# One softmax block left in PSUM, and one weight split in fixed slots, in an attention-and-Fourier kernel

## The chip, the cores and the metric

One core of a Trainium2 chip. A core has a matrix engine (TensorE), three engines for elementwise work (VectorE, ScalarE and GpSimd), a SyncE queue that issues the DMAs, and two on-chip memories: SBUF, and PSUM, whose banks take the results of TensorE. Each engine runs its own list of instructions in order; engines wait for one another by semaphores. In the profile the engines are called PE (PEld for its weight loads), DVE, ACT, POOL and SP.

The metric is the device time of one execution in microseconds (us), less is better.

## What is computed

Two independent halves, whose results stand side by side in the output. `x` has 2048 rows and 576 columns in each.

```python
# A: attention with 32 heads of 18 columns, in 4 segments of 512 rows
for s in range(4):
    logits = einsum("bhqd,bhkd->bhqk", qs, ks) * scale + mask   # causal in the segment
    p = softmax(logits)
    a_dot = einsum("bhqk,bhkd->bhqd", p, vs)
    a_mem = (phi(qs) @ M) / (phi(qs) @ z + 1e-6)                # memory of earlier segments
    o = g * a_mem + (1 - g) * a_dot
    M, z = M + phi(ks).T @ vs, z + phi(ks).sum()
a = concat(o) @ wo
# B: real part of a two-dimensional Fourier transform by matrices
y = Cr @ (x @ Hr.T) - Ci @ (x @ Hi.T)
```

`Hr` and `Hi` (576x576) are the first and the second transform along the columns, `Cr` and `Ci` (2048x2048) along the rows.

## The kernel before the change

**Precision by splitting.** Most operands are held as two parts, a rounded `hi` and the rest `lo = raw - hi`. ScalarE makes `hi` by a copy, VectorE or GpSimd subtracts, and TensorE adds the products `hi*hi`, `hi*lo` and `lo*hi`.

**Stages.** Up to about 215 us the projections and the memories of the segments are computed. Then one long stage, until about 928 us, runs attention (`attention()`) and the Fourier half (`dense()`) side by side: both are generators that yield after a piece of work. The main loop takes one slot of attention, runs what is due, and then takes pieces of `dense()` until its share of planned time has caught up. Last comes the output projection.

**Order of the work.** The order of instructions on each engine is the order in which the program emits them; nothing reorders it. `later(n, fn)` emits `fn` after `n` further ticks of a clock, and the main loop ticks once a slot. `PLAN` maps a slot's number (8 times the pair and the slot in the pair) to functions that are emitted there, behind that slot's own work; `at(p, slot, fn)` in `right_operands` fills it, before the change for the output projection's operands alone.

**A pair.** Attention handles two heads in one pass of its loop over `p` (64 pairs, 8 slots each). It works as a pipeline: pass `p` starts the row minima of pair `p` and goes on with pairs `p-2`, `p-3` and `p-4` (`F_LAG`, `T_LAG`, `V_LAG`). A block triangle of 4x4 blocks is computed in three pieces, `kind` 0, 1 and 2.

- Even head: `s_fill` computes scores and VectorE takes the row minima (line 973). Later `t_fill` computes the transposed scores with these minima added, and ScalarE takes exponentials. For `kind` 1 and 2 it does so twice from the same PSUM bank: `hi` in 16 bits (L1053) and `f` in 32 bits (L1054). For `kind` 0 GpSimd masks `f` first. `t_lo` (L1068) makes `lo = f - hi`: VectorE for `kind` 0 and 1, GpSimd for `kind` 2. `pv` multiplies by the values.
- Odd head: `f_fill` computes scores and minima in one go, `f_exp` takes exponentials (L996), `f_split_hi` and `f_split_lo` (L1003, L1007) split them into `hl`, and `f_turn` transposes `hl` into `ptt` by a DMA (L1012), which `pv` uses a pass later.

**PSUM banks.** `bank()` hands out two banks with tag `s` and two with tag `t`, each in turn. In a pass the tag `t` is taken four times: `t_fill` kind 0, 1 and 2, and `f_fill` kind 0. So `f_fill` kind 0 gets the bank that `t_fill` kind 1 had, and `t_fill` kind 1 of the next pass the one that `f_fill` kind 0 had. The tag `s` goes round `s_fill` 0, 1, 2 and `f_fill` 1, 2. A matmul into a bank waits until the readers of its last contents are done.

**Order in a pass, on VectorE:** `t_lo` 0 of the even head behind it, `s_fill` 0, `s_fill` 1, `f_split_lo` (512 columns), `s_fill` 2, `f_fill` 1, `f_fill` 0, `f_fill` 2, `t_lo` 1, then `pv_out` (L1098 to L1107). The middle block's exponentials stand in the tile `pf` in SBUF between L1054 and L1068.

**The second transform's weights.** `dense()` first makes the column transforms of the 16 row tiles with `Hr` (`hidden`, L94), then 16 row transforms (`sequence`, L583 and L628 to L633), then the same with `Hi`. `Hi` comes in five blocks of 128 rows. In the first row transforms `h_load(1, k)` loads block `k` (L425), and one `sequence` later `h_split(1, k)` makes its parts through `split_wk`: copies on ScalarE (L130), and two ticks later the subtractions on VectorE (L124, or L126 and L127 for the last block, which has two halves of 64 rows).

**Row maxima.** `maxima`, `maxima_transpose` and two small DMAs (`qs<-mt`) bring the minima of the even heads into the operand of the transposed scores.

Of the kernel before, what the change touches and what calls it, by code (L numbers as in the profile page):

```python
# [12 lines left out]
F32 = mybir.dt.float32  # L13
# [3 lines left out]
AF = mybir.ActivationFunctionType  # L17
OP = mybir.AluOpType
# [7 lines left out]
SCALE = DH ** -0.5  # L26
LOWEST = -3.0e38
LIFT = 12.0 * math.log(2.0)
# [12 lines left out]
def infini_attention_and_fnet(ctx: ExitStack, tc: tile.TileContext, xT, wqk, w8, wv, wo, beta, xtT, cT, hT, out):  # L41
    nc = tc.nc
    act, dve, pool, pe = nc.scalar, nc.vector, nc.gpsimd, nc.tensor
# [44 lines left out]
    def later(n, fn, *a):  # L88
        due.setdefault(clock[0] + n, []).append((fn, a))
# [28 lines left out]
            act.activation(t, raw, AF.Copy)  # L118
            dve.tensor_tensor(t[64:], raw[64:], t[64:].bitcast(F32), OP.subtract)

    def split_wk(w, k, raw, wait=0):
        def low():
            if k < 4:
                dve.tensor_tensor(w[1][k], raw, w[0][k].bitcast(F32), OP.subtract)  # L124
            else:
                dve.tensor_tensor(w[2][:64], raw[:64], w[2][:64].bitcast(F32), OP.subtract)  # L126
                dve.tensor_tensor(w[3][64:], raw[64:], w[3][64:].bitcast(F32), OP.subtract)  # L127

        for t in (w[0][k],) if k < 4 else (w[2], w[3]):
            act.activation(t, raw, AF.Copy)  # L130
        if wait:
            later(wait, low)
        else:
            low()

    def load_w(src, cols, k):
        raw = sb.tile([P, cols], F32, name="raw", tag="raw", bufs=5)
        dma(raw, src[k])
        return raw

    def weight(mk):
        return [[mk() for _ in range(4)] for _ in range(2)] + [mk() for _ in range(2)]

    def wide_tile(cols):
        return lambda: wide.tile([P, cols], F32R, name="wide", tag="wide")
# [17 lines left out]
    raw = sb.tile([P, L], F32, name="raw", tag="raw", bufs=5)  # L163
# [8 lines left out]
    for k in range(1, 5):  # L172
        load_x(0, k)
        raw = load_w(wqk[:, :, :L], L, k)
# [6 lines left out]
    for k in range(5):  # L181
        if k < 2:
            raw = sb.tile([P, L], F32, name="r", tag="r", bufs=3)
            dma(raw, wqk[k, :, L:])
        else:
            raw = load_w(wqk[:, :, L:], L, k)
# [234 lines left out]
    HW, HRAW = {}, {}  # L421

    def h_load(ri, k):
        HRAW[ri, k] = sb.tile([P, D], F32, name="raw", tag="raw", bufs=5 if ri == 0 else 3)
        dma(HRAW[ri, k], hT[ri, k])  # L425

    def h_split(ri, k):
        if k == 0:
            HW[ri] = weight(wide_tile(D))
        split_wk(HW[ri], k, HRAW.pop((ri, k)), 2 * ri)  # L430

    c_raw, c_split, c_seen = {}, {}, set()
    CHUNKS = [c for ri in range(2) for c in
# [29 lines left out]
    def stacks(p_, i):  # L463
        qs_bufs.append(p_.tile([P, 4, L], BF16, name=f"qs{i}"))
        ks_bufs.append(p_.tile([P, 4, L], BF16, name=f"ks{i}"))
        pool.memset(ks_bufs[i].bitcast(F32)[96:], BF16_ONES)
# [97 lines left out]
    def bank(name, shape, dtype, tag):  # L564
        turns[tag] ^= 1
        return ps.tile(shape, dtype, name=name, tag=f"{tag}{turns[tag]}", bufs=1)
# [43 lines left out]
    def y_load(tt):  # L610
        if tt < NT:
            Y[tt] = sb.tile([P, D], F32, name="y", bufs=3)
            dma(Y[tt], yd[tt])
# [54 lines left out]
    def dense():  # L668
        for ri in range(2):
            for tt in range(NT):  # L670
                yield from hidden(ri, tt)
            if ri:
                y_load(0)
            for tt in range(NT):
                late = tt - 8
                if ri == 0 and 0 <= late < 5:
                    h_load(1, late)
                if ri == 0 and 1 <= late < 6:
                    h_split(1, late - 1)
                yield from sequence(ri, tt)  # L680

    O, LEFT, WO, TAIL = {}, {}, {}, {}
# [11 lines left out]
            else:  # L694
                o_load(t, lambda: sr.tile([P, 5, P], F32, name="craw", bufs=4))

    PLAN = {}

    def right_operands():
        raw, late = {}, {}  # L700

        def at(p, slot, fn, *a):
            PLAN.setdefault(8 * p + slot, []).append((fn, a))

        def load(k):
            raw[k] = wide.tile([P, D], F32, name="wide", tag="wide") if k == 3 else sb.tile([P, D], F32, name="raw", tag="raw", bufs=3)
            dma(raw[k], wo[k])
# [241 lines left out]

    sq = ctx.enter_context(tc.tile_pool(name="sb2q", bufs=1, side="right", reuse_waits="tile"))  # L950
    sa = ctx.enter_context(tc.tile_pool(name="sb2a", bufs=1, reuse_waits="tile"))
    PT, PV = {}, {}

# [74 lines left out]
    def t_fill(n, kind, maxima_of=None):  # L1030
        G, h = divmod(n, 4)
        q, k = qs_bufs[G % 4][:NPAIR + 3, h], ks_bufs[G % 4][:NPAIR + 3, h]
        if kind == 0:
            PT[n] = (sa.tile([P, 1280], F16, name="phi", bufs=2), sa.tile([P, 1280], F16, name="plo", bufs=2),
                     sa.tile([P, 1280], F32, name="pf", bufs=3))
        hi, lo, f = PT[n]
        o = bank("t", [P, L], F32, "t")
        if kind == 0:
            for j in range(4):
                b = slice(j * P, (j + 1) * P)  # L1040
                pe.matmul(o[:, b], k[:, b], q[:, b], start=True, stop=True)  # L1041
            r, w = 0, 512
        elif kind == 1:
            pe.matmul(o[:, :384], k[:, :128], q[:, 128:], start=True, stop=True)
            if maxima_of is not None:
                maxima_transpose(maxima_of, o)
            r, w = 512, 384
        else:
            pe.matmul(o[:, 256:384], k[:, 256:384], q[:, 384:], start=True, stop=True)
            pe.matmul(o[:, :256], k[:, 128:256], q[:, 256:], start=True, stop=True)  # L1050
            r, w = 896, 384
        if kind:
            act.activation(hi[:, r:r + w], o[:, :w], AF.Exp, bias=LIFT, scale=SCALE)  # L1053
        act.activation(f[:, r:r + w], o[:, :w], AF.Exp, bias=LIFT, scale=SCALE)  # L1054

    def t_mask(n):
        v = PT[n][2][:, :512].rearrange("p (j q) -> p j q", j=4)
# [7 lines left out]
    def t_lo(n, kind):  # L1065
        hi, lo, f = PT[n]
        a, b = ((0, 512), (512, 896), (896, 1280))[kind]
        (pool if kind == 2 else dve).tensor_tensor(lo[:, a:b], f[:, a:b], hi[:, a:b], OP.subtract)  # L1068

    def pv(n):  # L1070
        G, h = divmod(n, 4)
# [71 lines left out]
    F_LAG, T_LAG, V_LAG = 2, 3, 4  # L1143
# [3 lines left out]
    def attention():  # L1147
        for p in range(NP + V_LAG):
            def even(lag, fn, *a):
                if 0 <= p - lag < NP:  # L1150
                    fn(2 * (p - lag), *a)

            def odd(lag, fn, *a):
                if 0 <= p - lag < NP:
                    fn(2 * (p - lag) + 1, *a)

            if p < 2:
                OG.append(sa.tile([P, 4, 72], F32, name=f"og{p}"))
            if p == 0:
                stack_load(1)  # L1160
                later(20, value_load, 0)
            if p % 2 == 0:
                later(39, value_load, p // 2 + 1)
                later(30, memory_load, p // 2)
            even(T_LAG + 1, t_lo, 0)
            odd(F_LAG + 1, f_exp, 2)
            odd(F_LAG + 1, f_split_hi)
            yield SLOTS[0]
            G = p // 2 - 1 if p % 2 == 0 and 0 < p <= NP else None
            even(0, s_fill, 0)  # L1170
            even(T_LAG, t_fill, 0)
            even(T_LAG, t_fill, 1, G)
            if G is not None and p < T_LAG:
                maxima_transpose(G, bank("trm", [P, L], F32, "t"))
            odd(F_LAG + 1, f_split_lo, pool, 512, 1280)
            yield SLOTS[1]
            even(0, s_fill, 1)
            odd(F_LAG + 1, f_split_lo, dve, 0, 512)
            yield SLOTS[2]
            even(V_LAG, pv)  # L1180
            if p < 2:
                stacks(sq, p + 2)
            even(0, s_fill, 2)
            even(T_LAG, t_mask)
            yield SLOTS[3]
            odd(F_LAG, f_fill, 1)
            even(T_LAG, t_fill, 2)
            odd(F_LAG, f_fill, 0)
            if p % 2 and p < NP:
                maxima(p // 2)  # L1190
            yield SLOTS[4]
            odd(F_LAG + 1, f_turn)
            if p % 2:
                if p == 1:
                    later(6, stack_load, 2)
                else:
                    stack_load((p + 3) // 2)
                if 2 < p < 18:
                    later(2, copy_parts, 2, 7 + p // 2)
            elif 4 <= p < 36:  # L1200
                later(2, copy_parts, 3, (p - 4) // 2)
            even(T_LAG, t_hi)
            yield SLOTS[5]
            odd(V_LAG, pv)
            odd(F_LAG, f_fill, 2)
            odd(F_LAG, f_exp, 1)
            even(T_LAG, t_lo, 1)
            even(T_LAG, t_lo, 2)
            yield SLOTS[6]
            odd(F_LAG, f_exp, 0)  # L1210
            if V_LAG <= p < NP + V_LAG - 1:
                pv_out(p - V_LAG)
            yield SLOTS[7]
# [8 lines left out]
    for n, w in enumerate(attention()):  # L1222
        tick()
        ta += w
        for fn, a in PLAN.pop(n, ()):
            fn(*a)
# [61 lines left out]
```

## Time and profile before

| | us |
|---|---|
| median of 3 runs | 988.1 |
| the three runs | 987.11, 988.10, 988.16 |
| the profiled execution | 987.47 |
| its span, first to last instruction | 985.7 |

Busy times of all engines, in stretches of the span (us):

| stretch | TensorE | VectorE | ScalarE | GpSimd | DMA share |
|---|---|---|---|---|---|
| 0 to 215 | 213.9 | 145.3 | 144.1 | 137.6 | 0.63 |
| 215 to 400 | 185.0 | 135.1 | 137.8 | 129.0 | 0.80 |
| 400 to 575 | 174.9 | 151.0 | 141.0 | 126.5 | 0.99 |
| 575 to 660 | 85.0 | 69.3 | 69.0 | 61.6 | 0.80 |
| 660 to 880 | 218.4 | 200.7 | 168.3 | 164.8 | 1.00 |
| 880 to 985 | 101.4 | 84.7 | 54.2 | 56.3 | 0.65 |

A row of a group reads: line, engine, operation, what it writes and reads, shape, count | busy time in us and mean ns of one | idle time of the engine just before it and what ended that. A row of a timeline reads: start in us, duration in us, engine, line, operation; in brackets the idle time before it. A row of one line's instructions gives minimum, median and maximum in ns. The matmuls of TensorE overlap, and their ends are modelled, so the distance from one start to the next says more than a duration.

### The profile page before, as it was taken

The page shows a single profiled execution, that of the slowest core. Times are in us where ns is not written, and L with a number is a line of the kernel's source. Part 1 is how long each engine was busy: PE and PEld are TensorE (multiplying, and loading weights), DVE is VectorE, ACT ScalarE, POOL GpSimd, SP SyncE. Part 2 cuts the span into 40 slices and gives each one's busy share as a digit, 9 for nine tenths or more (in the row PEclk, how much of TensorE's full clock was granted, in tenths as well). Part 3 has the DMA queues.
Part 4 walks back from the last instruction along what each step waited for, and adds up shares of the span by engine and source line. Part 5 has one row for each costly group of instructions (what it writes and reads, how often), then busy time and mean ns, then how long its engine had stood idle before and what let it go on. Part 6 is the DMA issues. An engine that isn't in the chain of part 4 may idle for free.

```text
span 985.7 us, 25490 instructions
## 1 busy us (share of the span) xinstructions
PE 978.7 (99%) x9246; PEld 917.6 (93%) x9246; DVE 786.1 (80%) x2113; ACT 714.3 (72%) x1687; POOL 675.7 (69%) x746
## 2 busy tenths in 40 slices
PE   9999999999999999999999999999999999999998
PEld 8989989899999999999999999999999989999998
DVE  6657668594678777887898888888888999999885
ACT  6757576664887877878878788886778867778442
POOL 2658577686767677666776777767677977767561
PEclk9999999999999999999999999999999999999999
DMA  7537557766778898899999997779999999988663
GB/s 237 199 117 238 203 172 249 239 238 189 185 186 218 206 253 221 214 236 237 243 239 229 228 217 189 186 199 217 239 220 247 242 225 257 233 200 191 169 197 116
DMA packets 304350, 209.96 MB, mean 213 GB/s; under 512 B 204992, under 2 KB 259136, under 8 KB 304192
## 3 DMA queue, kind: packets, MB, share of 16 engines
q1 hardware_dynamic: 304000, 208.20, 82.1%
q8 instruction: 72, 1.18, 0.5%
q14 instruction: 54, 0.44, 0.2%
q10 hardware_dynamic: 224, 0.14, 0.0%
HBM read 122.37 MB, written 58.98 MB: 184 GB/s over the span
## 4 chain that ended last, share of the span: by engine, by line
PE 94%; DVE 3%; DMA 1%; ACT 1%; issue 1%; POOL 0%; SPq 0%
PE d L583 38%; PE s L967 7%; PE v L84 6%; PE qk L84 6%; PE qk L250 6%; PE pv L1085 4%; PE d L628 3%; PE d L629 3%; PE d L630 3%; PE t L867 2%; PE pv L1086 2%; PE d L867 2%; PE s L867 1%; PE m L363 1%; PE t L1041 1%; PE look L396 1%
## 5 line engine op out<-in xcount | busy, mean ns | idle before, releaser
L973 DVE CUSTOM_DVE_ANT_0 s<-s,causal 128x128 f32<-128x128 f32 (+3 forms) x512 | 248.3, 503 | 90.9 <-PE s L967 80.8
L456 POOL TENSOR_TENSOR clo<-craw,chi 128x512 fp32r<-128x512 f32 x159 | 220.9, 1389 | 86.8 <-ACT chi L451 61.0
L583 PE MATMUL d<-wide,chi 128*128 128x288 f32 x1408 | 261.8, 303 | 0.0
L583 PEld LDWEIGHTS d<-wide,chi 128*128 128x128 f32 x1408 | 210.6, 188 | 2.3 <-issue 0.9
L583 PE MATMUL d<-wide,clo 128*128 128x288 f32 x704 | 173.2, 313 | 0.0
L1007 POOL TENSOR_TENSOR hl<-pf,hl 128x768 f16<-128x768 f32 x64 | 112.6, 1759 | 63.8 <-ACT hl L1003 53.7
L967 PE MATMUL s<-ks,qs 108*128 108x128 bf16 (+3 forms) x512 | 132.9, 303 | 1.1 <-DVE negm L973 1.1
L1053 ACT ACTIVATE phi<-t 128x384 f16<-128x384 f32 x128 | 61.7, 482 | 99.7 <-PE t L1050 99.7
L996 ACT ACTIVATE pf<-s,nb 128x128 f32<-128x128 f32 (+3 forms) x256 | 128.3, 527 | 6.2
L1068 DVE TENSOR_TENSOR plo<-pf,phi 128x384 f16<-128x384 f32 (+1 forms) x128 | 124.8, 975 | 0.0
L583 PE MATMUL d<-ab,chi 128*128 128x288 f32 x640 | 123.3, 302 | 0.0
L583 PEld LDWEIGHTS d<-wide,clo 128*128 128x128 f32 x704 | 117.8, 189 | 1.9 <-issue 0.4
L1054 ACT ACTIVATE pf<-t 128x384 f32<-128x384 f32 (+1 forms) x192 | 99.4, 518 | 6.5 <-PE t L1041 6.3
L451 ACT ACTIVATE chi<-craw 128x512 fp32r<-128x512 f32 x160 | 100.2, 627 | 4.5 <-DMA craw<-cT 2.8
L583 PEld LDWEIGHTS d<-ab,chi 128*128 128x128 f32 x640 | 97.8, 188 | 0.5
L1003 ACT ACTIVATE hl<-pf 128x768 f16<-128x768 f32 (+1 forms) x128 | 87.4, 730 | 2.0
L583 PE MATMUL d<-ab,clo 128*128 128x288 f32 x320 | 83.0, 308 | 0.0
L628 PE MATMUL d<-wide,chi 128*128 128x288 f32 x256 | 81.4, 318 | 0.0
L629 PE MATMUL d<-wide,chi 128*128 128x288 f32 x256 | 75.6, 295 | 0.0
L630 PE MATMUL d<-wide,clo 128*128 128x288 f32 x256 | 75.5, 295 | 0.0
L1068 POOL TENSOR_TENSOR plo<-pf,phi 128x384 f16<-128x384 f32 x64 | 62.3, 974 | 14.9 <-ACT pf L1054 10.8
L1007 DVE TENSOR_TENSOR hl<-pf,hl 128x512 f16<-128x512 f32 x64 | 68.3, 1068 | 0.0
(285 smaller groups left out, 2518.8 us busy)
## 6 DMA issues: line engine op xcount, KB each, us to landing
craw<-cT SPq DMA_DIRECT2D x128, 256.0 KB
ks<-kd SPq DMA_DIRECT2D x32, 432.0 KB
qs<-qd SPq DMA_DIRECT2D x32, 432.0 KB
craw<-xtT SPq DMA_DIRECT2D x32, 320.0 KB
vd<-vs SPq DMA_DIRECT2D x16, 440.0 KB
vst<-vd SPq DMA_DIRECT2D x32, 220.0 KB
qd<-p SPq DMA_DIRECT2D x16, 384.0 KB
kd<-p SPq DMA_DIRECT2D x16, 384.0 KB
```

The source lines that it names most:

```text
L84: pe.matmul(o, a, b, start=n == 0, stop=n == len(terms) - 1)
L451: act.activation(hi, raw[:, :4], AF.Copy)
L456: engine.tensor_tensor(lo, raw[:, :4], hi.bitcast(F32), OP.subtract)
L583: pe.matmul(o[h], a, b[:, h * 288:h * 288 + 288], start=start, stop=stop)
L628: pe.matmul(o, xh[:, k], wl[k][:, cs], start=k == 0, stop=False)
L629: pe.matmul(o, xh[:, k], wh[k][:, cs], start=False, stop=False)
L630: pe.matmul(o, xl[:, k], wh[k][:, cs], start=False, stop=False)
L967: pe.matmul(o[:, c:c + w], q[:, i * P:w], k[:, :w], start=True, stop=True)
L973: dve.tensor_tensor_reduce(o[:, c:c + w], o[:, c:c + w], CAUSAL[0][:, L - w:], scale=scale, scalar=-LOWEST, op0=OP.add, op1=OP.min, accum_ ...
L996: act.activation(f[:, FIRST_COL[i]:FIRST_COL[i] + w], o[:, c:c + w], AF.Exp, bias=nb[:, i:i + 1], scale=-1.0)
L1007: engine.tensor_tensor(hl[:, 1, a:b], f[:, a:b], hl[:, 0, a:b], OP.subtract)
L1068: (pool if kind == 2 else dve).tensor_tensor(lo[:, a:b], f[:, a:b], hi[:, a:b], OP.subtract)
```

## The change

It has two parts.

The middle block: for `kind` 1, ScalarE writes the 32-bit exponentials over the scores in their PSUM bank instead of into `pf`, and `t_lo` 1 reads them there. The call of `t_lo` 1 moves from behind `f_fill` 2 to behind `s_fill` 1 of the same pass.

The weights: `h_split(1, k)` is no longer called from `dense()`; it stands in `PLAN` at slot 2 of pairs 21, 23, 25, 27 and 29. The subtraction follows three ticks later, and for the last block the second half's eight ticks after the first half's. The loads stay where they were. For the first transform (`ri` 0) and for all other weights `split_wk` emits the same as before.

```diff
-    def split_wk(w, k, raw, wait=0):
-        def low():
+    def split_wk(w, k, raw, planned=False):
+        def low(i):
             if k < 4:
                 dve.tensor_tensor(w[1][k], raw, w[0][k].bitcast(F32), OP.subtract)
             else:
-                dve.tensor_tensor(w[2][:64], raw[:64], w[2][:64].bitcast(F32), OP.subtract)
-                dve.tensor_tensor(w[3][64:], raw[64:], w[3][64:].bitcast(F32), OP.subtract)
+                r = slice(64 * i, 64 * i + 64)
+                dve.tensor_tensor(w[2 + i][r], raw[r], w[2 + i][r].bitcast(F32), OP.subtract)
...
-        if wait:
-            later(wait, low)
-        else:
-            low()
+        for i in range(1 + k // 4):
+            if planned:
+                later(3 + 8 * i, low, i)
+            else:
+                low(i)
...
-        split_wk(HW[ri], k, HRAW.pop((ri, k)), 2 * ri)
+        split_wk(HW[ri], k, HRAW.pop((ri, k)), ri)
...
-                if ri == 0 and 1 <= late < 6:
-                    h_split(1, late - 1)
                 yield from sequence(ri, tt)
...
-    PLAN = {}
+    PLAN, HW1 = {}, 21
...
+        for k in range(5):
+            at(HW1 + 2 * k, 2, h_split, 1, k)
...
-        act.activation(f[:, r:r + w], o[:, :w], AF.Exp, bias=LIFT, scale=SCALE)
+        to = f[:, r:r + w]
+        if kind == 1:
+            to = KEPT[n] = o[:, :w]
+        act.activation(to, o[:, :w], AF.Exp, bias=LIFT, scale=SCALE)
...
-        (pool if kind == 2 else dve).tensor_tensor(lo[:, a:b], f[:, a:b], hi[:, a:b], OP.subtract)
+        f = KEPT.pop(n) if kind == 1 else f[:, a:b]
+        (pool if kind == 2 else dve).tensor_tensor(lo[:, a:b], f, hi[:, a:b], OP.subtract)
...
             even(0, s_fill, 1)
+            even(T_LAG, t_lo, 1)
             odd(F_LAG + 1, f_split_lo, dve, 0, 512)
...
             odd(F_LAG, f_exp, 1)
-            even(T_LAG, t_lo, 1)
             even(T_LAG, t_lo, 2)
```

More of the change, by code (lines that the diff above doesn't have):

```diff
@@ L951, in infini_attention_and_fnet @@
     sa = ctx.enter_context(tc.tile_pool(name="sb2a", bufs=1, reuse_waits="tile"))
-    PT, PV = {}, {}
+    PT, PV, KEPT = {}, {}, {}
     ROWS = (((3, 0),), ((0, 384), (2, 0)), ((1, 0),))
```

## The prediction

> **What bounds the kernel now.** I read the page first, for the engine that has no room, then the waits of TensorE, then single steps of its timeline.
>
> ```profile
> span 985.7 us, 25490 instructions
> PE 978.7 (99%) x9246; PEld 917.6 (93%) x9246; DVE 786.1 (80%) x2113; ACT 714.3 (72%) x1687; POOL 675.7 (69%) x746
> PE 94%; DVE 3%; DMA 1%; ACT 1%; issue 1%; POOL 0%; SPq 0%
> ...
> PE s L967 <- DVE negm L973: 1.1, 3, 0.4
> PE t L1041 <- DMA qs<-mt: 0.8, 1, 0.8
> ```
>
> TensorE is busy for 978.7 of 985.7 us and makes 94% of the chain of waits. Behind its start, only two kinds of wait are long enough to show as idle time: 1.1 us for VectorE and 0.8 us for one small DMA. The change removes no matmul, so it can shorten the program only through TensorE's waits. Idle time understates them, since ends of matmuls are modelled; starts are better. In TensorE's timeline:
>
> ```profile
> 666.12 0.18 PE L1086 MATMUL pv<-vst,plo 128*128 128x37 bf16 x1
> 666.68 0.27 PE L967 MATMUL s<-ks,qs 108*128 108x256 bf16 x1 [0.38 <-DVE negm L973]
> ...
> 810.20 0.20 PE L1085 MATMUL pv<-vst,phi 128*128 128x55 bf16 x1
> 810.39 0.19 PE L1086 MATMUL pv<-vst,plo 128*128 128x37 bf16 x1
> 810.43 0.19 PE L1085 MATMUL pv<-vst,phi 128*128 128x55 bf16 x1
> ...
> 810.87 0.18 PE L1086 MATMUL pv<-vst,plo 128*128 128x37 bf16 x1
> 811.42 0.27 PE L967 MATMUL s<-ks,qs 108*128 108x256 bf16 x1 [0.38 <-DVE negm L973]
> ...
> 862.72 0.30 PE L583 MATMUL d<-wide,chi 128*128 128x288 f32 x1
> 862.85 0.29 PE L583 MATMUL d<-wide,clo 128*128 128x288 f32 x1
> 863.19 0.38 PE L967 MATMUL s<-ks,qs 108*128 108x128 bf16 x2
> ...
> 882.84 0.18 PE L1086 MATMUL pv<-vst,plo 128*128 128x37 bf16 x1
> 883.37 0.27 PE L967 MATMUL s<-ks,qs 108*128 108x256 bf16 x1 [0.35 <-DVE negm L973]
> ```
>
> A small `pv` matmul is followed after about 0.03 us (810.39 to 810.43 is 0.04, most are less). The steps 666.12 to 666.68, 810.87 to 811.42 and 882.84 to 883.37 are 0.56, 0.55 and 0.53, so each holds about 0.5 us of waiting for VectorE's row minimum. The step 810.20 to 810.39 holds about 0.16 of waiting for `plo`. A `d` matmul takes 0.13 (862.72 to 862.85); the step to 863.19 is 0.34, 0.21 too long. Sum of what VectorE costs here: 0.53 + 0.52 + 0.50 + 0.16 + 0.21 = 1.92 us. Read the same way, I find no other wait on VectorE above 0.16 us between 215 and 930 us. The room for gain is small from the start.
>
> **VectorE's subtraction of the middle block, 64 times (`t_lo` with kind 1).** Groups by line with shapes kept apart, then single lines with minimum, median and maximum in ns:
>
> ```profile
> L1068 DVE TENSOR_TENSOR plo<-pf,phi 128x384 f16<-128x384 f32 x64 | 51.5, 804 | 0.0
> L276 DVE TENSOR_TENSOR r<-qk,p 128x512 f32<-128x512 f32 x36 | 24.6, 685 | 9.3 <-ACT p L275 7.7 <-POOL p L288 1.5
> ...
> L1054 ACT ACTIVATE pf<-t 128x384 f32<-128x384 f32 x128 | 61.9, 483 | 0.0
> ...
> L1068 DVE TENSOR_TENSOR plo<-pf,phi x128: 552/685/2164, 257.5 to 920.0; 128x384 f16<-128x384 f32 x64, 128x512 f16<-128x512 f32 x64
> L94 DVE TENSOR_TENSOR wide<-d,wide x44: 419/451/459, 221.8 to 625.3; 128x288 fp32r<-128x288 f32 x44
> ```
>
> It reads two SBUF tiles now: mean 804 ns, and the line spreads from 552 to 2164. Afterwards one operand lies in PSUM. No row of before has this form at 384 columns. L94 and L276 do, at 288 and 512, and L94 never leaves 419 to 459. Between them, 451 + 96/224 × (685 − 451) = 551 ns. Bounds: 0.45 (the shorter L94) and 0.80 (no change). I take 0.55, which is also the undisturbed minimum of today's form. So 0.25 × 64 = 16 us of VectorE's 786 go; off the path they are worth nothing.
> [...]
>
> ScalarE's write goes to PSUM: no row prices a ScalarE write there. Bounds 483 ± 130 ns, the upper above the 595 or so of 512 columns, or ± 8 us over 64 instructions. ScalarE's slack in the next fence hides it; I take nothing.
>
> **Its new place.** An ordinary pair, rows of VectorE, TensorE, ScalarE and SyncE:
>
> ```profile
> 441.05 0.14 DVE L973 DVE_READ_ACCUMULATOR2_ANT negm<- 128x1 f32 x1
> 441.05 0.70 DVE L1007 TENSOR_TENSOR hl<-pf,hl 128x512 f16<-128x512 f32 x1
> 443.85 0.14 DVE L973 DVE_READ_ACCUMULATOR2_ANT nb<- 128x1 f32 x1
> 444.95 0.43 DVE L973 CUSTOM_DVE_ANT_0 s<-s,causal 128x256 f32<-128x256 f32 x1 [0.96 <-PE s L967]
> 445.30 0.56 DVE L1068 TENSOR_TENSOR plo<-pf,phi 128x384 f16<-128x384 f32 x1
> ...
> 442.29 0.38 PE L967 MATMUL s<-ks,qs 108*128 108x512 bf16 x1
> 454.61 0.20 PE L1085 MATMUL pv<-vst,ptt 128*128 128x55 bf16 x1
> ...
> 438.98 0.50 ACT L1054 ACTIVATE pf<-t 128x384 f32<-128x384 f32 x1
> 442.49 0.49 ACT L1053 ACTIVATE phi<-t 128x384 f16<-128x384 f32 x1 [2.49 <-PE t L1050]
> 446.31 0.19 ACT L993 ACTIVATE nb<-nb 128x1 f32<-128x1 f32 x1
> ...
> 441.84 4.20 SPq L1012 DMA_TRANSPOSE ptt<-hl  x1
> ```
>
> The subtraction leaves 445.30, behind `f_fill` kind 2, and goes to 441.19, between `s_fill` kind 1 and `f_split_lo`. Its inputs are there since 439.48. Behind it wait, 0.55 later each: `f_split_lo`; the minima of `s_fill` 2, `f_fill` 1 and 0, up to 443.99; and through `hl` the transposing DMA, so SyncE's queue behind 441.84. The cover: VectorE idles 0.96 before 444.95, so the next minimum starts on time; ScalarE takes up `f_fill` 0's result only at 446.31, 2.3 us after it; the transposed block lands by about 446 and is used at 454.61. Price nothing; without cover 0.55 a pair.
>
> TensorE gets a new wait. `f_fill` kind 0 (442.29) reuses the bank with the middle block, so it must follow the subtraction instead of the exponential: 441.19 + 0.55 + about 0.06 for the signal (estimate) = 441.80, still 0.49 early. Where VectorE is late this margin shrinks:
>
> ```profile
> 661.18 1.62 DVE L1068 TENSOR_TENSOR plo<-pf,phi 128x384 f16<-128x384 f32 x1
> 805.06 1.17 DVE L1068 TENSOR_TENSOR plo<-pf,phi 128x384 f16<-128x384 f32 x1
> 884.08 0.14 DVE L973 DVE_READ_ACCUMULATOR2_ANT negm<- 128x1 f32 x1
> ...
> 884.67 0.38 PE L967 MATMUL s<-ks,qs 108*128 108x512 bf16 x1
> ```
>
> At 884 it is 0.45, below the 0.61 needed. But lateness is what the move removes: 1.62 us (661.18) and 1.17 us (805.06) of subtraction precede the stalls at 666 and 811 on VectorE's queue and would be gone before them; 0.8 on the mean elsewhere, more than any stall above. I take all 1.92 us off, and add 0.3 for new waits (bounds 0 and 1.2, the shortfalls of the 9 of 61 pairs whose margin is under 0.61, as at 884, if VectorE were no earlier at all).
>
> **The second transform's weights.** Same six ScalarE copies and six VectorE subtractions; their loads stay in the transform's loop.
>
> ```profile
> 520.79 1.25 ACT L130 ACTIVATE wide<-raw 128x576 fp32r<-128x576 f32 x2
> ...
> L124 DVE TENSOR_TENSOR wide<-raw,wide x4: 751/1690/1831, 452.1 to 505.0; 128x576 fp32r<-128x576 f32 x4
> ...
> 430.71 0.41 SPq L425 DMA_DIRECT2D raw<-hT  x1
> ```
>
> The copies come after pair 21's first scores, about 440, 9 us after the first load, and lie in front of 442.49, where ScalarE idles 2.49 us: 1.25 is hidden. The subtractions move to just before `f_fill` 2, where 0.96 us is idle: of 1.83 at most 0.87 spills over, against 0.80 that left the place behind it. Splitting the last block parts 2 × 1.5 us. None of the five stalls lies among 452 to 526, so I take nothing: bounds −0.3 (small waits) to +0.5 (one stall as at 666).
>
> **Sum.** Profiled execution 987.47 us (span 985.7 and 1.8 around it): 987.47 − 1.92 + 0.3 = 985.85. The median of the runs is 0.63 above this execution, their lowest value 0.36 below it; with half of the offset, 986.1.
>
> **Rivals.** First, **the waits are dealt anew**: VectorE's subtractions from two SBUF tiles, up to 2164 ns (L1068), fall elsewhere against GpSimd's work, and the 1.9 us come back at other pairs. For it: the other two such subtractions of each pair stay. Against: each pair has 0.25 us less of them. Time 987.47, with the same half offset 987.8.
>
> Second, on the other side, **the held bank**: `f_fill` 0 waits for VectorE. It decides once the subtraction ends later than the margin. If it stays at 0.80 and VectorE is no earlier, 0.86 is needed; 17 of the 61 pairs have less, as at 884 (0.45, 0.41 short), together 4.3 us. Then 987.8 + 4.3 = 992.1. For it: 0.45 at 884. Against: the ordinary 1.10 (441.19 to 442.29) and L94's steady 451 ns.
> [...]
>
> Third, **more than VectorE's waits go**: the earlier minima also spare the 0.8 us for `qs<-mt`: 987.8 − 1.92 − 0.8 = 985.1. Against: that DMA waits in SyncE's queue, which the change does not shorten.
>
> That **nothing is saved per subtraction** (0.80 in PSUM too) would still leave the move: the ordinary pair's margin of 1.10 holds 0.86, and with the new waits at their upper bound, 1.2 instead of 0.3, the time is 987.0, the end of the forecast's own range.
>
> **Numbers.** 0.2% is 2 us, about what a measurement of this kernel tells from no change. Forecast 0.57, own range 985.3 to 987; first rival 0.23, the held bank 0.14, the third 0.06. The forecast lies on the 2 us boundary below 988.1 (986.1): half of it counts as faster. Faster 0.29 + 0.06 + 0.05 from the first rival's spread of about ± 1 = 0.40; slower 0.14 and a little = 0.15; same 0.45. Range: 984.9 (just past the third rival) to 989.2, between the first rival and the held bank, which alone is left out.
>
> **What would show it.** Right: the group of 384 columns on VectorE at about 0.55 us; no step over 0.3 us before `s L967`; idle of 0.4 us or more left before the 256-column minimum. Wrong: TensorE waiting for `plo` at a 512-column `s`; ScalarE's PSUM write over 0.6 us; the same total of waits at other pairs; or a changed time with unchanged waits of TensorE.

## The result, and the profile after

| | before | after |
|---|---|---|
| median of 17 runs, us | 987.46 | 984.88 |
| lowest and highest, us | 985.94 to 988.44 | 984.28 to 986.89 |
| ratio, with its 95% interval | | 0.998 (0.9974 to 0.9987) |
| profiled execution, us | 987.47 | 984.37 |

The changed kernel is faster by about 0.2%: 2.6 us by the medians, with an interval that excludes no change. Of all runs of this document one, of the weights alone, took 1582.61 us at a granted clock of 0.557, and no figure below contains it. The page of the profile after:

```profile
span 982.7 us, 25421 instructions
...
PE 976.7 (99%) x9246; PEld 915.9 (93%) x9246; DVE 757.3 (77%) x2113; ACT 715.9 (73%) x1687; POOL 658.6 (67%) x746
...
PE 99%; DMA 0%; DVE 0%; ACT 0%; issue 0%; DVEq 0%
```

TensorE now makes 99% of the chain, where it made 94%; VectorE's 3% and the DMAs' 1% are gone from it. VectorE is busy for 28.8 us less than before (786.1 − 757.3), GpSimd for 17.1 us less; of these, 12.5 are its 159 `clo` subtractions of 512 columns, which were not touched (1389 to 1311 ns on the mean). What TensorE still waits for behind the start:

```profile
PE warm L240 <- DVE ones L68: 1.1, 1, 1.1
PE d L584 <- DVE ab L94: 0.3, 1, 0.3
```

The three waits for the row minimum and the wait for `qs<-mt` are gone, and there is one new wait. Now the groups by line with shapes kept apart, of after (line numbers are up by 1 to 6: L1068 is L1074, L1054 is L1059, L967 is L969, L583 is L584):

```profile
L1074 DVE TENSOR_TENSOR plo<-pf,phi 128x512 f16<-128x512 f32 x64 | 58.3, 910 | 0.0
...
L1074 DVE TENSOR_TENSOR plo<-t,phi 128x384 f16<-128x384 f32 x64 | 35.4, 554 | 7.2 <-ACT t L1059 6.5 <-issue 0.6
L1059 ACT ACTIVATE pf<-t 128x384 f32<-128x384 f32 x64 | 31.1, 486 | 0.0
L1059 ACT ACTIVATE t<-t 128x384 f32<-128x384 f32 x64 | 30.8, 481 | 0.0
```

and the row of before, in the same view, for the subtraction of 512 columns:

```profile
L1068 DVE TENSOR_TENSOR plo<-pf,phi 128x512 f16<-128x512 f32 x64 | 73.3, 1145 | 0.0
```

The middle block's subtraction fell from 804 to 554 ns (16.1 us in all). The other one, of 512 columns (`t_lo` 0), fell from 1145 to 910 (15.0 us) though neither its form nor its operands were touched: it only comes earlier, because the middle block's no longer stands in front of it. The traces show what the earlier place changes. In before, 56 of the 64 fall on work of GpSimd and take 1211 ns on the mean, and 43 of them fall mainly on its own subtraction of 768 columns for `hl`; the 8 during which GpSimd does nothing take 684 to 685. In after 53 fall on its work, with a mean of 957, and 28 of them mainly on that subtraction; the other 11 take 681 to 686. Together the two falls are VectorE's 28.8 us and some. The timeline shows both, at an ordinary pair, at the former stall of 666 us, and at the new wait:

```profile
440.46 0.55 DVE L1074 TENSOR_TENSOR plo<-t,phi 128x384 f16<-128x384 f32 x1
...
442.46 0.38 PE L969 MATMUL s<-ks,qs 108*128 108x512 bf16 x1
...
662.88 0.68 DVE L1074 TENSOR_TENSOR plo<-pf,phi 128x512 f16<-128x512 f32 x1
664.40 0.69 DVE L975 CUSTOM_DVE_ANT_0 s<-s,causal 128x512 f32<-128x512 f32 x1
...
666.08 0.18 PE L1092 MATMUL pv<-vst,plo 128*128 128x37 bf16 x1
666.11 0.27 PE L969 MATMUL s<-ks,qs 108*128 108x256 bf16 x1
...
288.20 1.45 DVE L1009 TENSOR_TENSOR hl<-pf,hl 128x512 f16<-128x512 f32 x1
289.57 0.45 DVE L94 TENSOR_TENSOR ab<-d,ab 128x288 fp32r<-128x288 f32 x1
...
289.51 0.30 PE L584 MATMUL d<-wide,clo 128*128 128x288 f32 x1
290.07 0.53 PE L584 MATMUL d<-wide,chi 128*128 128x288 f32 x2 [0.27 <-DVE ab L94]
```

The same stall in before:

```profile
664.38 1.21 DVE L1068 TENSOR_TENSOR plo<-pf,phi 128x512 f16<-128x512 f32 x1
...
665.88 0.69 DVE L973 CUSTOM_DVE_ANT_0 s<-s,causal 128x512 f32<-128x512 f32 x1
```

At the ordinary pair the subtraction ends at 441.01, and the matmul into its bank starts 1.45 us later: the bank is free in time. At the former stall the 512-column minimum starts at 664.40 instead of 665.88, and TensorE's next step is 0.03 us (666.08 to 666.11) instead of 0.56. At 290 us a new wait has come: `hl`'s subtraction takes 1.45 us, `ab`'s stands behind it, and TensorE's step from 289.51 to 290.07 is 0.56 instead of the usual 0.13.

**One table for all kernels.** I read TensorE's steps in every run as the prediction did: of each step from one start to the next, what exceeds the usual step of the same two kinds of matmul, over the long stage only (from the first attention scores to the first matmul of the output projection, about 215 to 930 us), wherever the trace names what ended a wait. Sums in us, by what ended the wait; the last column is the stage less these sums:

| kernel | stage | VectorE | DMA | other | rest |
|---|---|---|---|---|---|
| before | 709.43 | 2.38 | 1.08 | 0.22 | 705.75 |
| before, second profile | 709.41 | 3.29 | 0 | 0.49 | 705.63 |
| after | 706.34 | 0.53 | 0 | 0.22 | 705.59 |
| after, second profile | 707.96 | 0.53 | 1.61 | 0.22 | 705.60 |
| after, third profile | 706.33 | 0.52 | 0 | 0.22 | 705.59 |
| middle block alone | 707.98 | 2.14 | 0.03 | 0.22 | 705.59 |
| weights alone | 708.49 | 2.71 | 0 | 0.22 | 705.56 |
| new place, in SBUF | 711.12 | 3.13 | 1.43 | 0.22 | 706.34 |
| new place, in SBUF, weights planned | 709.07 | 1.74 | 1.09 | 0.22 | 706.02 |
| after, last block alone planned | 707.13 | 0.52 | 0.61 | 0.22 | 705.78 |
| after, bank held longer | 726.21 | 19.67 | 0 | 0.22 | 706.32 |
| after, work put back | 712.13 | 5.44 | 0 | 0.71 | 705.98 |
| after, maxima on ScalarE's queue | 705.87 | 0.10 | 0 | 0.22 | 705.55 |
| the same again | 706.70 | 0.09 | 0.91 | 0.22 | 705.48 |

The rest stays within 0.9 us while the stage moves by 20: the kernels differ mainly through TensorE's waits. The four highest rests (705.98 to 706.34) belong to the two kernels with the new place in SBUF, to the held bank and to the work put back; this part of their loss is put down to no wait. In the two profiles of before the waits for VectorE are 2.4 and 3.3; in the three of after 0.52 to 0.53, always the wait at 290 us (0.43) and one of 0.10 at 241. That is the gain. The waits for DMAs come and go from one execution to the next of one and the same kernel.

### The profile page after: what moved, and what is told of

Read it like the earlier page. It is cut to its first block, busy times and chain, and to the rows that moved or that the text cites. A ratio compares the mean times of both kernels' runs of the same rounds, so it can differ in the third digit from the quotient of the medians.

```text
span 982.7 us, 25421 instructions
## 1 busy us (share of the span) xinstructions
PE 976.7 (99%) x9246; PEld 915.9 (93%) x9246; DVE 757.3 (77%) x2113; ACT 715.9 (73%) x1687; POOL 658.6 (67%) x746
## 4 chain that ended last, share of the span: by engine, by line
PE 99%; DMA 0%; DVE 0%; ACT 0%; issue 0%; DVEq 0%
PE d L584 42%; PE s L969 7%; PE v L84 6%; PE qk L84 6%; PE qk L251 6%; PE pv L1091 4%; PE d L629 3%; PE d L630 3%; PE d L631 3%; PE t L869 2%; PE pv L1092 2%; PE d L869 2%; PE s L869 2%; PE t L1043 1%; PE m L364 1%; PE look L397 1%
## 5 line engine op out<-in xcount | busy, mean ns | idle before, releaser
L457 POOL TENSOR_TENSOR clo<-craw,chi 128x512 fp32r<-128x512 f32 x159 | 208.4, 1311 | 94.1 <-ACT chi L452 69.8
L584 PE MATMUL d<-wide,chi 128*128 128x288 f32 x1408 | 261.6, 303 | 0.3 <-DVE ab L94 0.3
L584 PEld LDWEIGHTS d<-wide,chi 128*128 128x128 f32 x1408 | 210.6, 188 | 1.8 <-DVE ab L94 0.5
L584 PE MATMUL d<-wide,clo 128*128 128x288 f32 x704 | 173.2, 313 | 0.0
L969 PE MATMUL s<-ks,qs 108*128 108x128 bf16 (+3 forms) x512 | 132.9, 303 | 0.0
L584 PE MATMUL d<-ab,chi 128*128 128x288 f32 x640 | 123.3, 302 | 0.0
L584 PEld LDWEIGHTS d<-wide,clo 128*128 128x128 f32 x704 | 117.8, 189 | 1.4
L584 PEld LDWEIGHTS d<-ab,chi 128*128 128x128 f32 x640 | 97.8, 188 | 0.5
L584 PE MATMUL d<-ab,clo 128*128 128x288 f32 x320 | 83.0, 308 | 0.0
L1059 ACT ACTIVATE pf<-t 128x512 f32<-128x512 f32 (+1 forms) x128 | 68.6, 536 | 5.8 <-PE t L1043 5.7
L1074 POOL TENSOR_TENSOR plo<-pf,phi 128x384 f16<-128x384 f32 x64 | 61.0, 953 | 15.4 <-ACT pf L1059 12.6
L1074 DVE TENSOR_TENSOR plo<-pf,phi 128x512 f16<-128x512 f32 x64 | 58.3, 910 | 0.0
```

The costliest lines, as they stand in the source:

```text
L457: engine.tensor_tensor(lo, raw[:, :4], hi.bitcast(F32), OP.subtract)
L584: pe.matmul(o[h], a, b[:, h * 288:h * 288 + 288], start=start, stop=stop)
L969: pe.matmul(o[:, c:c + w], q[:, i * P:w], k[:, :w], start=True, stop=True)
L1074: (pool if kind == 2 else dve).tensor_tensor(lo[:, a:b], f, hi[:, a:b], OP.subtract)
```

## The experiments

**Before, once more** (no edit), and **after, twice more** (no edit), to see what one profile is worth.

> The kernel before once more, for a second profile. If the waits are the program's own, those for VectorE stand at the same places within 0.05 us each (666, 811, 883), and so does the wait of 0.96 us for the small DMA at 797. If the DMA's wait is chance, it is missing or elsewhere.

Time 987.51, span 985.8. The only entry in the list of TensorE's waits behind the start:

```profile
PE s L967 <- DVE negm L973: 0.7, 2, 0.4
```

The three waits for the row minimum that the prediction found are there again, at 667.23, 811.26 and 883.46 us, with 0.53, 0.29 and 0.49 by starts; new ones of 0.2 to 0.3 have come at 524 (for ScalarE), 527, 759, 761 and 822 us, and the wait for the DMA at 797 us has not. So the prediction's list was in part that of one execution: the three stalls recur, two of them with the same amount and the one at 811 with half of it, and other waits come and go.

> The changed kernel once more, for a second profile. Theory (its program leaves TensorE hardly any waits for VectorE, and the small DMA's waits are chance): waits for VectorE 0.4 to 0.7 us in all, the one at 290 among them; for the DMA anything from 0 to 1.1 us. If the first profile was a lucky one, waits for VectorE of 1 us or more.

Time 985.92, 1.55 above the first profile of after, and the waits say why:

```profile
PE t L1043 <- DMA qs<-mt: 1.3, 2, 0.7
...
PE d L584 <- DVE ab L94: 0.3, 1, 0.3
```

The wait for `qs<-mt` was not removed by the change; the first profile of after merely had none.

> The changed kernel, timed on the same chip as e11_maxima_queue_again, for a direct comparison. Ratio to the kernel before 0.9974 to 0.9987 as measured first; waits for the small DMA between 0 and 1.6 us in the trace, as in its two profiles so far.

984.90 us (984.55 to 985.80, 11 runs), ratio 0.9979 (0.997 to 0.9987): the result repeats, and the third profile has the same 0.52 us of waits for VectorE as the first.

**Each part alone.** Middle block alone: after, but with the weights as in before.

```diff
...
-        split_wk(HW[ri], k, HRAW.pop((ri, k)), ri)
+        split_wk(HW[ri], k, HRAW.pop((ri, k)), 2 * ri)
...
+                if ri == 0 and 1 <= late < 6:
+                    h_split(1, late - 1)
...
-        for k in range(5):
-            at(HW1 + 2 * k, 2, h_split, 1, k)
```

`split_wk` itself is that of before, too.

> The middle block as in the change, the second transform's weights as before. Theory (the gain is TensorE's waits for VectorE, taken away by moving the subtraction ahead): nearly all of the gain stays, 2 to 2.8 us under the kernel before (ratio 0.9970 to 0.9985); in the trace no step over 0.3 us before a score matmul of 256 columns. Rival (the gain comes from the planned weights): within 0.5 us of the kernel before.

986.35 us, ratio 0.9993 (0.9985 to 1.0002): less than half of the gain (0.94 us below the 987.29 of before in the same set of runs), against nearly all of it as expected: the weights do count. Of its 2.14 us of waits for VectorE, 0.77 and 0.84 lie at one pair, 29, where the last block of the weights falls. The timeline of this kernel there:

```profile
521.18 1.24 ACT L130 ACTIVATE wide<-raw 128x576 fp32r<-128x576 f32 x2
523.17 0.49 ACT L1057 ACTIVATE t<-t 128x384 f32<-128x384 f32 x1
...
523.70 0.56 DVE L1072 TENSOR_TENSOR plo<-t,phi 128x384 f16<-128x384 f32 x1 [1.47 <-ACT t L1057]
524.77 1.85 DVE L126 TENSOR_TENSOR wide<-raw,wide 64x576 fp32r<-64x576 f32 x1
526.64 0.76 DVE L127 TENSOR_TENSOR wide<-raw,wide 64x576 fp32r<-64x576 f32 x1
527.42 0.43 DVE L973 CUSTOM_DVE_ANT_0 s<-s,causal 128x256 f32<-128x256 f32 x1
...
524.31 0.38 PE L967 MATMUL s<-ks,qs 108*128 108x512 bf16 x1 [0.61 <-DVE plo L1072]
528.01 0.27 PE L967 MATMUL s<-ks,qs 108*128 108x256 bf16 x1 [0.69 <-DVE negm L973]
```

The two copies of the weights stand on ScalarE just ahead of the exponential into the bank. It ends at 523.66 (523.17 + 0.49), the subtraction that frees the bank at 524.26, and `f_fill` 0 starts at 524.31: the held bank, at one pair. Then both halves' subtractions, 1.85 and 0.76 us, stand ahead of the minimum that TensorE needs for its next scores. In after the same stretch runs thus:

```profile
521.67 0.49 ACT L1059 ACTIVATE t<-t 128x384 f32<-128x384 f32 x1
522.08 1.25 ACT L130 ACTIVATE wide<-raw 128x576 fp32r<-128x576 f32 x2
...
525.16 0.74 DVE L127 TENSOR_TENSOR wide<-raw,wide 64x576 fp32r<-64x576 f32 x1
526.75 0.43 DVE L975 CUSTOM_DVE_ANT_0 s<-s,causal 128x256 f32<-128x256 f32 x1 [0.84 <-PE s L969]
```

The fixed slot puts the copies behind the exponential, and of the two halves only one lies ahead of this minimum, for which VectorE is now idle 0.84 us.

Weights alone: after, but with the middle block's exponentials in SBUF and its subtraction in its old place.

```diff
-        to = f[:, r:r + w]
-        if kind == 1:
-            to = KEPT[n] = o[:, :w]
-        act.activation(to, o[:, :w], AF.Exp, bias=LIFT, scale=SCALE)
+        act.activation(f[:, r:r + w], o[:, :w], AF.Exp, bias=LIFT, scale=SCALE)
...
-            even(T_LAG, t_lo, 1)
             odd(F_LAG + 1, f_split_lo, dve, 0, 512)
...
+            even(T_LAG, t_lo, 1)
             even(T_LAG, t_lo, 2)
```

> The weights planned as in the change, the middle block as before. Theory: no gain, within 0.5 us of the kernel before (ratio 0.9995 to 1.0005), and the waits of about 0.5 us before score matmuls of 256 columns are there as before. Rival (the gain comes from the weights): 1.5 to 2.6 us faster.

987.23 us (median of eleven runs), ratio 1.0001 (0.9992 to 1.001). Alone the weights bring nothing that can be measured: the waits at 666.88, 810.54 and 882.71 us are all there (0.53, 0.31, 0.51).

Last block alone: after, but with blocks 0 to 3 of the weights split from `dense()` as before.

```diff
...
+                if ri == 0 and 1 <= late < 5:
+                    h_split(1, late - 1)
...
-        for k in range(5):
-            at(HW1 + 2 * k, 2, h_split, 1, k)
+        at(HW1 + 8, 2, h_split, 1, 4)
```

> The changed kernel, but only the last block of the weights is planned and split in two; the first four are as before. Theory (the weights part does no more than take away the two waits, 0.77 and 0.84 us, that the last block causes in e1_middle_only at 524 and 528 us): as fast as the changed kernel within 0.5 us, ratio to the kernel before 0.9970 to 0.9987. Rival (all five blocks count): halfway between e1_middle_only and the changed kernel, 0.9985 to 0.9992.

985.55 us, ratio 0.9978 (0.997 to 0.9987): the ratio of the whole change, with the same 0.52 us of waits for VectorE. Of the second part only the last block counts.

**The place apart from PSUM.** New place alone: before, with `t_lo` 1 moved and nothing else.

```diff
             even(0, s_fill, 1)
+            even(T_LAG, t_lo, 1)
             odd(F_LAG + 1, f_split_lo, dve, 0, 512)
...
-            even(T_LAG, t_lo, 1)
             even(T_LAG, t_lo, 2)
```

> The subtraction of the middle block moved as in the change, but its exponentials stay in SBUF; weights as before. Theory that the place counts: 1.2 to 2.4 us faster than before (ratio 0.9976 to 0.9988), the subtraction still at 0.8 us on the mean. Rival that the PSUM operand counts (out of GpSimd's way): no gain, ratio 0.9995 or more, since disturbed subtractions of up to 2 us now stand in front of three row minima.

989.90 us, ratio 1.0024 (1.0015 to 1.0034): slower than before. The theory that the place gives the gain falls. Its waits:

```profile
PE t L1041 <- DMA qs<-mt: 1.1, 2, 0.9
PE s L967 <- DVE negm L973: 1.1, 1, 1.1
PE d L583 <- DVE ab L94: 0.6, 1, 0.6
```

The stalls of 666, 811 and 883 us are gone, but the one behind the last block of the weights is the largest (1.1; by starts 1.21, at 528 us), and `ab` is late. Its groups of `t_lo` 0 and of the middle block:

```profile
L1068 DVE TENSOR_TENSOR plo<-pf,phi 128x512 f16<-128x512 f32 x64 | 58.1, 908 | 0.0
L1068 DVE TENSOR_TENSOR plo<-pf,phi 128x384 f16<-128x384 f32 x64 | 55.2, 862 | 8.6 <-ACT pf L1054 7.9 <-issue 0.6
```

In SBUF the subtraction costs more in the new place than in the old (862 against 804 ns). `t_lo` 0 takes 908 ns as in after: its fall comes from the place and not from the PSUM operand. VectorE is busy for 7.2 us less than before (778.9), and the kernel is still slower; what counts is which matmul waits.

Both parts in SBUF: after, but with the exponentials written to `pf`.

```diff
-        to = f[:, r:r + w]
-        if kind == 1:
-            to = KEPT[n] = o[:, :w]
-        act.activation(to, o[:, :w], AF.Exp, bias=LIFT, scale=SCALE)
+        act.activation(f[:, r:r + w], o[:, :w], AF.Exp, bias=LIFT, scale=SCALE)
...
-        f = KEPT.pop(n) if kind == 1 else f[:, a:b]
-        (pool if kind == 2 else dve).tensor_tensor(lo[:, a:b], f, hi[:, a:b], OP.subtract)
+        (pool if kind == 2 else dve).tensor_tensor(lo[:, a:b], f[:, a:b], hi[:, a:b], OP.subtract)
```

> Both parts of the change except that the middle block's exponentials stay in SBUF: the subtraction at the new place reads two SBUF tiles. It differs from e3_moved_in_sbuf only by the planned weights. Theory after the first four runs (the PSUM operand is what makes the new place bearable): 1.2 us or so better than e3_moved_in_sbuf, whose wait of 1.21 us at 528 falls away, so 0 to 1.6 us slower than before (ratio 1.000 to 1.0016). Rival (the place alone gives the gain once the weights are out of the way): 1.5 us or more faster than before.

987.22 us, ratio 0.9998 (0.999 to 1.0007): all of the change but the PSUM operand gains nothing. It is 2.7 us better than the new place alone (989.90), more than the 1.2 expected. The group of the middle block:

```profile
L1070 DVE TENSOR_TENSOR plo<-pf,phi 128x384 f16<-128x384 f32 x64 | 58.8, 919 | 7.2 <-ACT pf L1056 6.4 <-issue 0.6
```

919 ns against 554 from PSUM in the same place. The waits for VectorE are 1.74 us, at places where after has none or less: 0.75 at 291 us (`ab`), 0.33 at 589 and 0.42 at 776. With after beside it, the PSUM operand is worth 2.3 us (987.22 − 984.88, by medians of different sets of runs); 1.2 of these are waits for VectorE (1.74 and 0.53), the rest is not assigned.

The PSUM operand in the old place could not be had: there the subtraction stands behind `f_fill` 0's minimum on VectorE, while `f_fill` 0 would have to wait for the subtraction to free its bank. It was not tried.

**The held bank.** After, with the subtraction one step later, behind `f_split_lo`.

```diff
             even(0, s_fill, 1)
-            even(T_LAG, t_lo, 1)
             odd(F_LAG + 1, f_split_lo, dve, 0, 512)
+            even(T_LAG, t_lo, 1)
```

> The change with the subtraction one place later, behind the split of the odd head's 512 columns: same work, bank held 0.7 to 1.1 us longer. Theory (the bank's margin decides): f_fill kind 0 waits where split + subtraction + signal exceed the margin; from the gaps of the changed kernel 39 of 61 pairs are short by 17 us together, less what VectorE catches up while TensorE waits: 6 to 17 us slower than the changed kernel. Rival (the bank is free in time anyway): within 0.5 us of the changed kernel.

1003.48 us, ratio 1.0166 (1.0153 to 1.0179), 18.6 us above after. The group of the 512-column scores:

```profile
L969 PE MATMUL s<-ks,qs 108*128 108x512 bf16 x128 | 49.2, 384 | 14.1 <-DVE plo L1074 13.6
```

TensorE waits for `plo` ahead of `f_fill` 0, as the second rival has it; by starts 19.67 us, nearly all of it ahead of 34 such matmuls. That is just beyond the 6 to 17 us expected. In the trace of after, the time from the subtraction's end to `f_fill` 0 is shorter than the split and 0.06 us for the signal at 38 of 63 pairs, by 17.9 us together (the 0.06 is the prediction's estimate; where TensorE waited for the subtraction in the middle block alone, its matmul started 0.05 us after it, 524.26 to 524.31); this kernel adds 19.1 us of waits (19.67 − 0.53), and its split takes 1241 ns on the mean, where that of after takes 1066.

**The work put back.** After, with a further subtraction of 384 columns between two SBUF tiles, whose result nobody uses, in the old place.

```diff
+    def t_again(n):
+        hi, lo, f = PT[n]
+        again = sa.tile([P, 384], F16, name="again", bufs=1)
+        dve.tensor_tensor(again, f[:, 896:], hi[:, 896:], OP.subtract)
...
             odd(F_LAG, f_exp, 1)
+            even(T_LAG, t_again)
             even(T_LAG, t_lo, 2)
```

> The changed kernel with one more subtraction of 384 columns from two SBUF tiles, into a tile that nothing reads, at the place that the middle block's subtraction left. Theory (a contended subtraction ahead of the next pass makes VectorE late, and TensorE waits for it): waits before score matmuls of 256 columns come back, 1 to 2.5 us over the changed kernel (ratio to the kernel before 0.999 to 1.001). Rival (VectorE has room enough, and the gain is only in how the held bank and the DMAs fall): within 0.5 us of the changed kernel.

990.00 us, ratio 1.0025 (1.0016 to 1.0034), 5.1 us above after: the direction as expected, the size more than twice. Groups, then the old stall:

```profile
L1074 DVE TENSOR_TENSOR plo<-pf,phi 128x512 f16<-128x512 f32 x64 | 77.4, 1209 | 0.0
L1079 DVE TENSOR_TENSOR again<-pf,phi 128x384 f16<-128x384 f32 x64 | 53.6, 837 | 0.0
```

```profile
662.68 1.64 DVE L1079 TENSOR_TENSOR again<-pf,phi 128x384 f16<-128x384 f32 x1
665.89 1.20 DVE L1074 TENSOR_TENSOR plo<-pf,phi 128x512 f16<-128x512 f32 x1
...
667.62 0.18 PE L1097 MATMUL pv<-vst,plo 128*128 128x37 bf16 x1
668.18 0.27 PE L969 MATMUL s<-ks,qs 108*128 108x256 bf16 x1 [0.37 <-DVE negm L975]
```

With a subtraction from SBUF back in front of it, `t_lo` 0 takes 1209 ns again (910 in after, 1145 in before), and the stall at 666 us is back at its old size, a step of 0.56 (now at 668); so are those of 811 and 883, at 812 and 885 us with 0.27 and 0.49. It is the work in front of `t_lo` 0, not the pair, that makes these stalls. The kernel has one subtraction a pair more than before, and waits elsewhere come on top.

**A version that goes further.** After, with the small DMAs of the row maxima issued from ScalarE's queue instead of SyncE's. In the second profile of after, SyncE's queue and the matmul that waits read:

```profile
782.61 4.83 SPq L1014 DMA_TRANSPOSE ptt<-hl  x1
...
790.43 1.53 SPq L94 DMA_DIRECT2D qs<-mt  x2
...
797.43 0.40 PE L1043 MATMUL t<-qs,ks 111*128 111x128 bf16 x4 [0.66 <-DMA qs<-mt]
```

```profile
787.51 0.25 ACT L1028 ACTIVATE mt<-t 24x128 bf16<-24x128 f32 x1
```

The maxima are ready at 787.76, but the DMAs are issued only at 790.43: the transposing DMA holds the queue until 787.44, and five others that it kept back follow until 790.37. In the first profile of after that transposing DMA began at 779.67, the small DMAs were issued at 787.68, and no matmul waited.

```diff
-            later(1, dma, qs_bufs[G % 4][NPAIR:NPAIR + 3, 2 * h].rearrange("c (n t) -> c n t", n=4), w[12 * h:12 * h + 12])
+            later(1, nc.scalar.dma_start, qs_bufs[G % 4][NPAIR:NPAIR + 3, 2 * h].rearrange("c (n t) -> c n t", n=4), w[12 * h:12 * h + 12])
```

> The changed kernel with the two small DMAs of the row maxima (qs<-mt) issued from ScalarE's queue instead of SyncE's, so that they no longer stand behind transposes and loads. If waits for that DMA are what is left to gain: none in the trace, 0 to 0.6 us faster than the changed kernel (ratio to the kernel before 0.9970 to 0.9982). Against: ScalarE's own instructions wait behind the issue; then equal or slower.

984.20 us, ratio 0.9968 (0.9956 to 0.9979). Behind the start no wait is left in the list:

```profile
PE warm L240 <- DVE ones L68: 1.1, 1, 1.1
```

> The kernel of e9_maxima_on_act_queue again, beside the changed kernel. If the small DMA's waits, 0 to 1.6 us, are what it takes away: 0.3 to 1.5 us faster than e10_after_timed by the medians, and no wait for that DMA in the trace. If its better ratio was the chip's: within 0.3 us.

984.45 us, ratio 0.9971 (0.9959 to 0.9982), beside 984.90 and 0.9979 for after on the same chip. Neither profile has a wait for `qs<-mt`, nor the one at 290 us, but behind the start of this one another DMA was late:

```profile
PE pv L1091 <- DMA ptt<-hl: 0.7, 1, 0.7
```

A difference of 0.45 us with overlapping intervals: a hint that this version is a little faster than after, not shown.

## Why the prediction was right, and where not

Forecast: 986.1 us, 2.0 below the median shown then. Measured: 984.88, 2.6 below the median of before in the same runs (987.46), and a hair under the range's low end of 984.9. The direction and its cause were right. The sum, made against the profiled execution, gave 985.85, and the profiled execution of after took 984.37. Of these 1.48 us, 1.08 are the DMA waits that this execution of after happened not to have, 0.23 are VectorE's (1.85 net against 1.92 − 0.3), the remaining 0.17 the rest of the stage.

- **"I take all 1.92 us off."** Right for the whole change: the waits at 666, 811 and 883 us, the 0.16 at 810 and the 0.21 at 863 are gone in all three profiles of after. What was not seen is that a part of them was that of one execution; the second profile of before had 3.3 us in place of 2.4. Nor does the middle block alone, to which the sum put down all of the gain, bring it: it gives 0.94 us. That the sum came out near is in part luck.
- **0.55 us for the subtraction from PSUM.** Right: 554 ns, and no longer uneven (545 to 559 over 64). The view of single lines of after:

```profile
L1074 DVE TENSOR_TENSOR plo<-t,phi x64: 545/553/559, 252.3 to 908.3; 128x384 f16<-128x384 f32 x64
...
L1074 DVE TENSOR_TENSOR plo<-pf,phi x64: 681/685/1890, 257.9 to 914.5; 128x512 f16<-128x512 f32 x64
```

  In before, 11 of the 64 subtractions of 384 columns ran while GpSimd did nothing, and took 552 to 557 ns; the other 53 took 553 to 1683, 856 on the mean. In after 62 of 64 fall on work of GpSimd, and none takes more than 559. So the PSUM operand makes it no dearer than the quiet SBUF form, and takes it out of GpSimd's way: from two SBUF tiles the same subtraction in the same place took 919 ns on the mean.
- **"0.25 × 64 = 16 us of VectorE's 786 go."** Right as a term (16.1), but "the other two such subtractions of each pair stay" was not: `t_lo` 0 also lost 15.0 us, by its earlier place. With the work put back in front of it, it is dear again (1209 ns).
- **ScalarE's write to PSUM: "I take nothing."** Right: 481 ns, beside 486 for the same instruction to SBUF in the same kernel.
- **"Lateness is what the move removes."** Only half right. The move takes the three stalls away, but with the operand in SBUF it brings others: alone it is slower than before (1.0024), with the weights planned it is even (0.9998). That is the first rival, "the waits are dealt anew", and the PSUM operand is what keeps it from happening. The forecast of 987.0 for "nothing is saved per subtraction" lies near the 987.22 of that kernel by chance: it reckons with 0.80 us and a held bank, and that kernel has 0.92 and holds none.
- **The held bank.** Right to fear, right not to expect: at the ordinary pair after has 1.45 us between the subtraction's end and the next use of the bank, and one instruction of VectorE in between costs 18.6 us. Its price was for a subtraction that stays at 0.80, which no run had with the bank held.
- **The weights: "None of the five stalls lies among 452 to 526, so I take nothing: bounds −0.3 … to +0.5."** This step failed. Alone they bring nothing indeed, but with the subtraction in its new place they take away two waits of 0.77 and 0.84 us at pair 29, which the middle block's part makes there: 1.5 us by medians (986.35 against 984.88 and 984.90). Only the first of the two is the held bank's; with the operand in SBUF the second is there too (1.21), and the planned weights bring 2.7 us (989.90 against 987.22). The step priced the two parts against the stalls of before, and not against each other. That the last block alone suffices shows where they meet: copies ahead of the exponential into the bank, and two halves' subtractions ahead of one minimum.
- **"0.3 for new waits".** 0.43 came, at 290 us, but by another way than the bank: `ab`'s low part behind a slow `hl`.
- **The third rival, the DMA wait gone too.** It came out so in the first profile, by chance: the second profile of after has 1.61 us of it, the second of before none.

## What to carry to other kernels

Where one engine is 99% busy, sum what its steps from start to start exceed their usual length, and take more than one execution of it before pricing single stalls. An operand that VectorE read from PSUM instead of a second SBUF tile made a subtraction short and even here, 554 ns (545 to 559) for 804 to 919; it holds the bank for longer, so the reading must be emitted ahead of everything that the bank's next user waits behind: one instruction of VectorE in between cost 18.6 us. Parts of a change that work on the same engines in the same pass are to be priced together: here each alone brought little or nothing, and the two together removed most of TensorE's waits for VectorE (0.5 us left of 2.4 and 3.3).

## What was not expected of the hardware

- A subtraction that was not touched got 20% cheaper by coming earlier (1145 to 910 ns), and dear again (1209) when another was put ahead of it. From two SBUF tiles its time depended on whether GpSimd worked meanwhile: in after 681 to 686 ns where it did not, up to 1890 where it did.
- ScalarE wrote 128x384 to PSUM in 481 ns and to SBUF in 486: no difference that would count.
- A transposing DMA took SyncE's queue for 4.83 us (from 782.61), and the issue of all that stood behind it moved back; from the issue of the small DMAs (790.43) to the start of the matmul that needed them passed another 7.0 us.
- The waits of TensorE for DMAs were 0 to 1.6 us in executions of one and the same kernel with the same order of instructions, and in after they are the whole difference between two profiled executions (984.37 and 985.92).
